# Linear attention and MLP, two layers: rows of M moved as whole words and split at their chunks, late q further ahead, k ahead of G

## The chip, the cores and the metric

The kernel runs on one core of a Trainium2 chip. The metric is the device time of one execution in microseconds. A core has five engines that run side by side, each through its own list of instructions in order: PE (TensorE, matmuls; its weight loads are shown apart as PEld), DVE (VectorE), ACT (ScalarE), POOL (GpSimd) and SP (SyncE, which here issues nearly all transfers). They wait for each other through semaphores. Transfers run on 16 DMA engines. Matmul results land in PSUM, which has eight banks; everything else lies in SBUF.

## The reference

Two layers, each a linear attention block and an MLP, on 2048 rows of width 640 (32 heads of 20), MLP width 1728, in float32:

```python
def _A_ref(x, wqkv, wo):
    q, k, v = ...
    phi = lambda t: jnp.where(t > 0, t + 1, jnp.exp(t)) + 1e-6
    pq, pk = phi(q), phi(k)
    kv = jnp.einsum("bhsd,bhse->bhde", pk, v)
    z = jnp.einsum("bhsd->bhd", pk)
    num = jnp.einsum("bhqd,bhde->bhqe", pq, kv)
    den = jnp.einsum("bhqd,bhd->bhq", pq, z)[..., None] + 1e-6
    ...
    return (num / den).reshape(B, S, D) @ wo

def _B_ref(x, w1, b1, w2, b2):
    h = jnp.einsum("bsd,df->bsf", x, w1) + b1
    r = jnp.where(h > 0, h, 0)
    return jnp.einsum("bsf,fd->bsd", r * r, w2) + b2

x = x + _A_ref(_layernorm(x), wqkv, wo)
x = x + _B_ref(_layernorm(x), w1, b1, w2, b2)
...
```

The last two lines run twice, once for each layer.

## The kernel before

The 2048 rows are 16 tiles of 128 rows. A float32 product is made of three matmuls in the type fp32r: each operand is split into a high part (a copy rounded to fp32r, mostly by ACT) and a low part (the operand less the high part, by DVE), and high by low, low by high and high by high are added up in PSUM (`mm3`, L379). So every operand costs a split, two instructions, before PE can use it.

**The loop over tiles** (L665 to L767) makes k, and for most tiles q, from the turned and normalised x (`part`, 15 matmuls for 320 columns). `Phi` applies the feature map in halves: an exponential on ACT (`exp`, L475) and two operations on DVE (`rest`, L482 and L483). v is never made; instead G = x^T phi(k) is summed over the tiles in five PSUM banks (`g_part`, five parts of three matmuls 512 wide for the tile before, handed out by `gs(n)`), and what doesn't fit there, the last 128 columns, is GT, made for two tiles at a time after every even tile (`gt_part`, two halves of six matmuls, each added into SBUF by DVE, L513). Three banks, XB = 0, 1, 2, serve k, q and GT. Tiles of `LATE` (9, 11 to 15 in layer 0; 8, 9, 11, 13 to 15 in layer 1) leave their q for later: k is made there in two halves, in banks 0 and 1. `k_post` splits phi(k) into kh (high on ACT, low on DVE at L653) and adds it to `acc` on POOL. `move` turns x: DVE turns blocks of 32x32 (L356) and ACT moves them to their places (L365, 16 small moves for a tile). These are also how other tiles are turned later.

**The stage around the change** (from L772). `late_q(n)` makes n of the 12 late parts (half a tile's q each): 15 matmuls, an exponential, the two operations of `rest`, and after a tile's second half a store of it. They fill PE while other engines prepare. Then: G is read out, the small block products per six heads are made (`kv_make`, masked to `kvbd`), and M = (block-diagonal kv) times wo, of 640 by 640, is made in six pieces of 120 rows (`m_make(c)`, c from 0 to 5, the last of 40 rows). PE later needs M in five chunks of 128 rows, so a piece has to move to other partitions: ACT writes the piece's high part (L868), DVE its low part (L869), and SP copies both, 5,120 bytes a row, with up to two transfers into the chunks that the piece crosses (L873, L875). Piece 0 needs no move, its rows are the first of chunk 0; chunk m then gets rows of pieces m and m + 1. Between the pieces the loop gives one entry of `side_work` at a time to ACT (`run_side`: a quarter of the moves that turn a tile of phi(q), or its split into pT), one step of `b_ops` to DVE (`b_step`: phi(q) times z, its sum per head, the division, the turning), and one late part after piece 2.

**Behind the loop** PE makes pT times M for tiles 0 and 1: chunks 0 to 2 of both tiles, then chunks 3 and 4 of both (`proj`). `x_turned(i)` adds the result to x (`b_x1`, L621), normalises and turns it; tiles 2 and 3 follow whole (`b_out`), with late parts between. Tiles 2 and 3 are turned by PE (`f_trans`), and with `f_split` xTb, the operand of the MLP's first product (`fc1`, L987), is complete for the first four tiles. The rest of a layer is the MLP over four groups of four tiles, into which the attention output of later tiles is woven.

Short tiles of 128x640 (`ftile`) share 12 buffers; tiles of both halves (`xtile`: xh, kh, pT, kvbd, and the pieces Mc) share 8 in each layer. The program's order on each engine is the order of the text.

Of the kernel before, what the change touches and what calls it, by code (L numbers as in the profile page):

```python
# [8 lines left out]
F32 = mybir.dt.float32  # L9
R32 = mybir.dt.float32r  # L10
AF = mybir.ActivationFunctionType
ALU = mybir.AluOpType
# [59 lines left out]
def kernel(  # L72
# [25 lines left out]
    def bank(i, n=1):  # L98
        return PS[:, 512 * i : 512 * (i + n)]
# [269 lines left out]
    def halves(ps):  # L369
        return ps.rearrange("p (b n) -> p b n", b=2)[:, :, :HD]  # L370

    def halves_sb(t):
        return t.rearrange("p (b n) -> p b n", b=2)
# [58 lines left out]
    for layer in range(N_LAYERS):  # L432
# [57 lines left out]
        def xtile(name, dtype=R32):  # L490
            return xp.tile([P, 2, D], dtype, tag="x", name=name, bufs=8)
# [12 lines left out]
        def gt_part(p, j, ps):  # L504

            ps, rs = ps[:, :HD], slice(j * HD, (j + 1) * HD)
            for t in (2 * p, 2 * p + 1):
                a, b = kh[t][:, :, DM:], xh[t][:, :, rs]
                mm3(ps, a[:, 0], a[:, 1], b[:, 0], b[:, 1], t % 2 == 0, t % 2 == 1)
            if p == 0:  # L510
                nc.vector.tensor_copy(GT_[:, rs], ps)
            else:
                nc.vector.tensor_tensor(out=GT_[:, rs], in0=ps, in1=GT_[:, rs], op=ALU.add)  # L513
# [151 lines left out]
        for t in range(NT):  # L665
            first = t == 0 and layer == 0
            early = t == 0 and layer > 0
            a_load(t + 3, src)
            if first:
                late_consts()  # L670
            if layer == 0:
                prep.store()
                if 6 <= t < 6 + 2 * DC:
                    keep_kq(*divmod(t - 6, 2))
            if t >= 13:
                b_load_pq(t - 13)
                load_vo(2 * t - 26)
                load_vo(2 * t - 25)
            if first:
                fk, fq = Phi(rtile()), Phi(rtile())  # L680
                for nm, f, pss in (("k", fk, (bank(0), bank(1))), ("q", fq, (bank(2), bank(7)))):
                    w = wk(nm)
                    for c in range(DC):
                        for j in range(2):
                            s = slice(j * HD, (j + 1) * HD)
                            mm3(
                                pss[j][:, :HD], xT[t][:, 0, c, :], xT[t][:, 1, c, :],
                                w[c][:, 0, s], w[c][:, 1, s], c == 0, c == DC - 1,
                            )
                        if nm == "q" and c == 2:  # L690
                            a_trans(1, bank(5, 2))
                            a_stats(2)
                            a_apply(2)
                    for j in range(2):
                        f.exp(j * HD, pss[j][:, :HD])
                    if nm == "k":
                        f.rest()
                xh[t] = split_new(xt[t], "xh")
                k_post(t, fk.r)
                fq.rest()  # L700
                nc.sync.dma_start(pqd[0], fq.r)
                continue
            g = list(range(DC)) if t > 0 else []

            def gs(n):
                for _ in range(min(n, len(g))):
                    g_part(t - 1, g.pop(0))

            if q_end:
                q_end()  # L710
                q_end = None
            is_late = t in late
            f, fq = Phi(rtile()), None if is_late else Phi(rtile())
            n0 = HD if is_late else 512
            ps = part(t, 0, n0, bank(XB[0]))
            gs(0 if t == 1 and layer == 0 else 2)
            move(t + 1)
            f.exp(0, ps)
            if layer == 0 and t == 1:
                a_stats(3)  # L720
                a_trans(2, bank(5, 2))
            if not early and t + 2 < NT:
                a_apply(t + 2)
                yza[t + 2] = blocks_T(xt[t + 2])
            f.rest()
            gt = t % 2 == 0 and t > 0
            if gt and is_late:
                gt_part(t // 2 - 1, 0, bank(XB[2]))
            ps = part(t, n0, D if is_late else 1024, bank(XB[1]))
            if t + 1 in yza:  # L730
                xT_split(t + 1, yza.pop(t + 1)[1])
            if early:
                xT_split(2, yz0[2][1])
            for _ in range(PREP.get(t, 0) if layer == 0 else 0):
                prep.high()
            for _ in range(4):
                prep.low()
            for _ in range(PREP.get(t + 1, 0) if layer == 0 else 0):
                prep.load()
            f.exp(n0, ps[:, : D - n0])  # L740
            if not is_late:
                fq.exp(0, ps[:, D - n0 :])
            f.rest()
            if not is_late:
                fq.rest()
            xh[t] = split_new(xt[t], "xh")
            if gt and not is_late:
                gt_part(t // 2 - 1, 0, bank(XB[0]))
            gs(1)
            if is_late:  # L750
                gs(1)
            else:
                ps = part(t, 1024, 2 * D, bank(XB[2]))
                gs(1)
            k_post(t, f.r, [lambda: a_stats(t + 3)])
            if gt:
                gt_part(t // 2 - 1, 1, bank(XB[2 if is_late else 1]))
            gs(DC)
            if not is_late:

                def q_end(t=t, f=fq, ps=ps):
                    f.exp(1024 - D, ps)
                    f.rest()
                    nc.sync.dma_start(pqd[t], f.r)

            move(t + 2, AHEAD)
# [8 lines left out]
        def late_q(n=1, rest=True):  # L775

            for _ in range(n):
                if not late_parts:
                    return
                t, j = late_parts.pop(0)  # L780
                if j == 0:
                    late_phi[t] = Phi(ftile("rl"))
                late_phi[t].exp(j * HD, part(t, D + j * HD, D + (j + 1) * HD))
                late_todo.append((t, j))
                if rest:
                    late_rest()
# [70 lines left out]
        def m_make(c):  # L857
            mb.append(mb.pop(0))
            ps = bank(mb[-1], 2)
            n, o = head_rows(c), HR * c  # L860
            for j in range(2):
                nc.tensor.matmul(
                    ps[:n, j * 512 : j * 512 + HD], kvbd[c][:n, :n],
                    vo["o", c][:n, j * HD : (j + 1) * HD], start=True, stop=True,
                )
            u = M[0] if c == 0 else xtile("Mc")
            hi, lo, src_ = halves_sb(u[:n, 0]), halves_sb(u[:n, 1]), halves(ps[:n])
            nc.scalar.activation(hi, src_, AF.Copy)  # L868
            nc.vector.tensor_tensor(out=lo, in0=src_, in1=hi.bitcast(F32), op=ALU.subtract)  # L869
            if c > 0:  # L870
                m, r = divmod(o, P)
                k = min(P - r, n)
                nc.sync.dma_start(M[m][r : r + k].bitcast(F32), u[:k].bitcast(F32))  # L873
                if k < n:
                    nc.sync.dma_start(M[m + 1][: n - k].bitcast(F32), u[k:n].bitcast(F32))  # L875

        for c in range(NH):
            kv_make(c)
            if c == 0:
                b_load_pq(3)  # L880
            if c == 1:
                b_load_x(0)
            if c == 3:
                b_load_x(1)
            if c == 2:
                run_side(1)
            if c < 4:
                b_step(2)
        sg.close()
        sm = ExitStack()  # L890
# [2 lines left out]
        )  # L893

        M = [mp.tile([P, 2, D], R32, tag="M", name="uM", bufs=DC) for _ in range(DC)]
        late_q(1)
        b_step(2, 9)
        side_moves(yzp[2], lambda: b_split(2, xtile("pT")))
        xbanks = [0, 1]
        for c in range(NH):  # L900
            m_make(c)
            run_side(1)
            b_step(3)
            if c == 2:
                late_q(1)
        side_moves(yzp[3], lambda: b_split(3, xtile("pT")))

        wu.free = 3
        wu.load_ring()
        late_q(1)  # L910
        run_side(1)

# [6 lines left out]
        for i in range(2):  # L921
            po[i] = bank(4 + 2 * i, 2)
            proj(po[i], pT[i], M, range(3))
            run_side(2)

        def x_turned(i):
# [7 lines left out]
            run_side(1)  # L934
            b_load_x(i + 2)
        x_turned(0)
        late_q(1)
        run_side(2)
        x_turned(1)

# [13 lines left out]
        late_q(1)  # L954
        run_side(9)
        f_trans(2, bank(6, 2))
        late_q(1)
        f_trans(3, bank(4, 2))
        late_q(9)
        sa.close()  # L960

        sb = ExitStack()
# [556 lines left out]
```

## Time and profile before

| | us |
|---|---|
| median of 3 runs (lowest to highest) | 1363.93 (1363.85 to 1364.41) |
| the profiled execution, whole | 1362.51 |
| its span, first to last instruction | 1360.3 |

How the lines below are read. A row of the timeline is: start in us from the span's start, duration in us (of all instructions of the row from the first start to the last end), engine, line of the kernel, operation, output<-inputs by the program's names, the engine's shape, the number of instructions merged, and in brackets how long the engine stood idle before and what ended it. SPq marks a transfer being issued. In a table of waits the three numbers are the total in us, how many times, and the longest. A row of windows gives for a stretch of time the busy us of PE, PEld, DVE, ACT and POOL with their instructions, then the granted clock of PE as a share, the mean busy share of the DMA engines, and GB/s. In the page's groups, the row ends with the group's busy time and mean duration and the idle time before it. "DMA to landing" is from the issue of a transfer to its completion: lowest, median, highest of the group.

### The profile page before, as it was taken

The numbers are of one execution on the slowest core, as the hardware profiler recorded it, in microseconds if no ns is written. First come the engines' busy times: TensorE is split into PE (matmuls) and PEld (weight loads), VectorE is DVE, ScalarE is ACT, GpSimd is POOL, SyncE is SP. The second block draws the span as 40 slices with busy tenths as digits, with TensorE's granted clock in tenths as the row PEclk, the third lists the DMA queues.
The fourth block names the chain that finished last, engine by engine and source line by source line (L and its number), as shares of the span: only waits on it lengthen the run. The fifth ranks groups of instructions, "written<-read, shape, count | busy, mean of one in ns | idle before, by whom it ended". The sixth has DMA issues, their size and how long they took to land.

```text
span 1360.3 us, 19010 instructions
## 1 busy us (share of the span) xinstructions
PE 1344.3 (99%) x6817; PEld 1161.5 (85%) x6817; DVE 910.4 (67%) x1617; ACT 770.8 (57%) x1931; POOL 122.8 (9%) x174
## 2 busy tenths in 40 slices
PE   9999998999999999999999999989999999999998
PEld 8888987988888888888888898978888888888887
DVE  7888766777777676643467676757778667775323
ACT  5888857666646447411447687475756446464110
POOL 2222210000000000000012232100000000000000
PEclk9999999999999999999999999999999999999999
DMA  6787825583664484387521114175546646644834
GB/s 203 252 301 268 285 82 172 200 306 119 230 242 157 160 303 165 113 328 295 183 97 54 44 47 148 40 243 224 183 159 224 223 144 220 249 158 142 290 122 158
DMA packets 85635, 256.10 MB, mean 188 GB/s; under 512 B 11030, under 2 KB 19606, under 8 KB 84902
## 3 DMA queue, kind: packets, MB, share of 16 engines
q1 hardware_dynamic: 85398, 254.70, 53.1%
q8 instruction: 54, 0.88, 0.3%
q14 instruction: 39, 0.32, 0.1%
q10 hardware_dynamic: 144, 0.20, 0.0%
HBM read 193.50 MB, written 56.03 MB: 183 GB/s over the span
## 4 chain that ended last, share of the span: by engine, by line
PE 93%; ACT 3%; DMA 2%; DVE 1%; issue 0%; SPq 0%; POOL 0%; DVEq 0%
PE PS L379 36%; PE PS L987 27%; PE PS L1037 27%; ACT z L365 2%; DMA uM<-Mc 1%; PE PS L849 1%; ACT Mc L868 0%; DMA st<-in_A_wqkv_dram 0%; ACT e L475 0%; PE PS L1051 0%; DVE r L483 0%; DVE kq L128 0%; ACT xTb L127 0%; DVE e L482 0%; ACT kh L646 0%
## 5 line engine op out<-in xcount | busy, mean ns | idle before, releaser
L365 ACT ACTIVATE z<-y 32x160 f32<-32x160 f32 x1424 | 475.8, 334 | 73.8 <-DVE y L356 57.5
L987 PE MATMUL PS<-xTb,u 128*128 128x512 f32 x1400 | 333.8, 390 | 0.6 <-DVE xTb L128 0.6
L987 PEld LDWEIGHTS PS<-xTb,u 128*128 128x128 f32 x1400 | 261.6, 188 | 54.6 <-DVE xTb L128 1.1
L379 PE MATMUL PS<-kq,xT 128*128 128x320 f32 (+2 forms) x1635 | 296.1, 333 | 1.0 <-DVE kq L128 0.9
L379 PEld LDWEIGHTS PS<-kq,xT 128*128 128x128 f32 x1635 | 260.1, 188 | 28.7 <-DVE kq L128 1.1
L1037 PE MATMUL PS<-u,h 128*128 128x512 f32 x1120 | 276.8, 390 | 0.0
L1037 PEld LDWEIGHTS PS<-u,h 128*128 128x128 f32 x1120 | 208.5, 188 | 40.8
L999 ACT ACTIVATE hr<-PS,b1sb 128x512 f32<-128x512 f32 x104 | 71.4, 687 | 296.8 <-PE PS L987 296.1
L1000 DVE TENSOR_TENSOR hr<-hr 128x512 f32<-128x512 f32 x104 | 71.7, 690 | 219.1 <-ACT hr L999 218.5
L379 PE MATMUL PS<-kh,xh 128*128 128x512 f32 x480 | 126.0, 393 | 0.8 <-DVE kh L653 0.8
L475 ACT ACTIVATE e<-PS 128x320 f32<-128x320 f32 (+4 forms) x128 | 53.8, 436 | 115.0 <-PE PS L379 111.8
L379 PE MATMUL PS<-uM,pT 128*128 128x320 f32 x648 | 104.9, 312 | 8.2 <-DMA uM<-Mc 8.2
L379 PEld LDWEIGHTS PS<-uM,pT 128*128 128x128 f32 x648 | 99.3, 190 | 11.0 <-issue 7.9
L340 POOL TENSOR_SCALAR rs<-mv 128x1 f32<-128x1 f32 x64 | 28.2, 441 | 874.9 <-DVE mv L338 874.9
L379 PEld LDWEIGHTS PS<-kh,xh 128*128 128x128 f32 x480 | 86.9, 188 | 16.1 <-DVE kh L653 1.6
L482 DVE TENSOR_SCALAR e<-e 128x320 f32<-128x320 f32 (+4 forms) x128 | 41.1, 321 | 77.4 <-ACT e L475 77.2
L1037 PE MATMUL PS<-h,u 128*128 128x512 f32 x280 | 79.0, 390 | 0.0
L1002 DVE TENSOR_TENSOR h<-hr,h 128x512 fp32r<-128x512 f32 x104 | 72.0, 693 | 3.6
L650 POOL TENSOR_TENSOR acc<-acc,r 128x640 f32<-128x640 f32 x30 | 53.9, 1796 | 204.8 <-DVE r L483 204.8
L1037 PEld LDWEIGHTS PS<-h,u 128*128 128x128 f32 x280 | 52.2, 188 | 10.8 <-DVE h L1013 0.4
L987 PE MATMUL PS<-xTb,uw 128*128 128x512 f32 x240 | 57.0, 389 | 0.0
L483 DVE SCALAR_TENSOR_TENSOR r<-PS,e 128x512 f32<-128x512 f32 (+2 forms) x104 | 51.1, 492 | 5.8 <-ACT e L475 2.4
(119 smaller groups left out, 1336.2 us busy)
## 6 DMA issues: line engine op xcount, KB each, us to landing
u<-kept_w SPq DMA_DIRECT2D x184, 640.0 KB, 4.1
x<-x SPq DMA_DIRECT2D x48, 320.0 KB, 5.1
kept_w<-uprep SPq DMA_DIRECT2D x23, 640.0 KB, 4.5
pqt<-pq SPq DMA_DIRECT2D x32, 320.0 KB, 4.3
x<-xr SPq DMA_DIRECT2D x32, 320.0 KB, 4.1
st<-in_B_w_dram SPq DMA_DIRECT2D x22, 320.0 KB, 5.7
pq<-r SPq DMA_DIRECT2D x20, 320.0 KB
kept_kq<-kq SPq DMA_DIRECT2D x10, 640.0 KB, 6.7
```

Of the source, the lines that this page charges most:

```text
L340: nc.gpsimd.tensor_scalar(rs, mv[:, 1:2], LN_EPS, None, op0=ALU.add)
L365: nc.scalar.activation(zv[j * B32 : (j + 1) * B32, :, i, :], yv[i * B32 : (i + 1) * B32, :, j, :], AF.Copy)
L379: nc.tensor.matmul(ps, a, b, start=first and i == 0, stop=last and i == 2)
L475: nc.scalar.activation(self.e[:, a:b], ps, AF.Exp)
L482: nc.vector.tensor_scalar(e, e, 1.0, PHI_EPS, op0=ALU.min, op1=ALU.add)
L483: nc.vector.scalar_tensor_tensor(out=self.r[:, a:b], in0=ps, scalar=0.0, in1=e, op0=ALU.max, op1=ALU.add)
L650: nc.gpsimd.tensor_tensor(out=acc, in0=acc, in1=r, op=ALU.add)
L987: nc.tensor.matmul(ps, a[:, d, :], bb[:, d, :], start=d == 0 and i == 0, stop=d == DC - 1 and i == len(seq) - 1,)
L999: nc.scalar.activation(r, ps, AF.Relu, bias=b1sb[:, c : c + 1])
L1000: nc.vector.tensor_tensor(out=r, in0=r, in1=r, op=ALU.mult)
L1002: nc.vector.tensor_tensor(out=h[:, 1], in0=r, in1=h[:, 0].bitcast(F32), op=ALU.subtract)
L1037: nc.tensor.matmul(ps, l, r, start=first and k == 0, stop=last and k == len(a) - 1)
```

## The change

Three edits. First, `m_make` no longer splits a piece: ACT copies it as float32 into one tile, and the transfers carry whole words, 2,560 bytes a row, into raw chunks `m_raw` (three tiles of the kind `xtile`, two chunks in each; a piece on its way is now an `ftile`). A new function `m_split(m)` makes chunk m's high part with a copy on DVE and its low part with a subtraction on DVE, once its rows are there. Second, the late parts behind the loop are placed otherwise: two parts, each with one entry of side work and one `m_split`, ahead of the ring's weight loads and of the first product with M; the part behind the first `x_turned` is gone; and the last two parts leave their `rest` until after the splits of x (`late_rest`). `b_step(2)` is called three times instead of four within the loop over `kv_make`. Third, in late tiles the second half of k follows the first directly: no part of G between them, and both halves of GT follow later, the second in bank XB[0] instead of XB[2], ahead of `k_post`.

```diff
-            gs(0 if t == 1 and layer == 0 else 2)
+            gs(0 if is_late or t == 1 and layer == 0 else 2)
...
-            if gt and is_late:
-                gt_part(t // 2 - 1, 0, bank(XB[2]))
             ps = part(t, n0, D if is_late else 1024, bank(XB[1]))
...
             gs(1)
             if is_late:
                 gs(1)
+                if gt:
+                    gt_part(t // 2 - 1, 0, bank(XB[2]))
+                gs(1)
+                if gt:
+                    gt_part(t // 2 - 1, 1, bank(XB[0]))
...
             k_post(t, f.r, [lambda: a_stats(t + 3)])
-            if gt:
-                gt_part(t // 2 - 1, 1, bank(XB[2 if is_late else 1]))
+            if gt and not is_late:
+                gt_part(t // 2 - 1, 1, bank(XB[1]))
...
-            u = M[0] if c == 0 else xtile("Mc")
-            hi, lo, src_ = halves_sb(u[:n, 0]), halves_sb(u[:n, 1]), halves(ps[:n])
-            nc.scalar.activation(hi, src_, AF.Copy)
-            nc.vector.tensor_tensor(out=lo, in0=src_, in1=hi.bitcast(F32), op=ALU.subtract)
+            u = m_raw[0] if c == 0 else ftile("Mc")
+            nc.scalar.activation(halves_sb(u[:n]), halves(ps[:n]), AF.Copy)
             if c > 0:
                 m, r = divmod(o, P)
                 k = min(P - r, n)
-                nc.sync.dma_start(M[m][r : r + k].bitcast(F32), u[:k].bitcast(F32))
+                nc.sync.dma_start(m_raw[m][r : r + k], u[:k])
                 if k < n:
-                    nc.sync.dma_start(M[m + 1][: n - k].bitcast(F32), u[k:n].bitcast(F32))
+                    nc.sync.dma_start(m_raw[m + 1][: n - k], u[k:n])
+
+        def m_split(m):
+            nc.vector.tensor_copy(M[m][:, 0], m_raw[m])
+            nc.vector.tensor_tensor(
+                out=M[m][:, 1], in0=m_raw[m], in1=M[m][:, 0].bitcast(F32), op=ALU.subtract
+            )
...
-            if c < 4:
+            if c < 3:
                 b_step(2)
...
+        m_raw = [xtile("Mr", F32) for _ in range(3)]
+        m_raw = [m_raw[m // 2][:, m % 2] for m in range(DC)]
...
             if c == 2:
                 late_q(1)
+            if c in (3, 4):
+                m_split(c - 3)
         side_moves(yzp[3], lambda: b_split(3, xtile("pT")))
+        late_q(1)
+        run_side(1)
+        m_split(2)
+        late_q(1)
+        run_side(1)
+        m_split(3)
 
         wu.free = 3
         wu.load_ring()
-        late_q(1)
-        run_side(1)
...
             proj(po[i], pT[i], M, range(3))
+            if i == 0:
+                m_split(4)
             run_side(2)
...
         x_turned(0)
-        late_q(1)
         run_side(2)
         x_turned(1)
...
         f_trans(2, bank(6, 2))
-        late_q(1)
+        late_q(1, False)
         f_trans(3, bank(4, 2))
-        late_q(9)
+        late_q(9, False)
+        late_rest()
```

## The prediction

> **What bounds the kernel now.** I read the page first, then the waits of the tensor engine, then the timeline around those waits. The page's first lines:
>
> ```profile
> span 1360.3 us, 19010 instructions
> PE 1344.3 (99%) x6817; PEld 1161.5 (85%) x6817; DVE 910.4 (67%) x1617; ACT 770.8 (57%) x1931; POOL 122.8 (9%) x174
> ```
>
> PE is the bound nearly everywhere. The change gives it the same matmuls as before, so it can only win or add holes. The table of PE's waits names them:
>
> ```profile
> PE PS L379 <- DMA uM<-Mc: 8.2, 4, 2.9
> PE PS L379 <- DVE kh L653: 0.8, 1, 0.8
> PE PS L987 <- DVE xTb L128: 0.6, 2, 0.3
> ```
>
> All three parts of the diff aim at these rows: M not yet in its chunks (8.2 us), kh late (0.8), the turned x late for the first product of the MLP (0.6). The place is the M stage of each layer; layer 0 first, layer 1 in the last three rows:
>
> ```profile
> 220.86 2.47 PE L379 MATMUL PS<-kq,xT 128*128 128x320 f32 x15
> 223.17 1.92 PE L379 MATMUL PS<-uM,pT 128*128 128x320 f32 x12
> 223.17 0.68 ACT L868 ACTIVATE Mc<-PS 40x640 fp32r<-40x640 f32 x1
> 224.04 0.81 DVE L869 TENSOR_TENSOR Mc<-PS,Mc 40x640 fp32r<-40x640 f32 x1
> 225.32 0.77 SPq L873 DMA_DIRECT2D uM<-Mc  x1
> 227.94 4.63 PE L379 MATMUL PS<-uM,pT 128*128 128x320 f32 x30 [2.85 <-DMA uM<-Mc]
> 234.07 2.87 PE L379 MATMUL PS<-uM,pT 128*128 128x320 f32 x18 [1.50 <-DMA uM<-Mc]
> 236.78 2.36 PE L379 MATMUL PS<-kq,xT 128*128 128x320 f32 x15
> 238.98 4.56 PE L379 MATMUL PS<-uM,pT 128*128 128x320 f32 x30
> 892.24 2.46 PE L379 MATMUL PS<-kq,xT 128*128 128x320 f32 x15
> 897.44 4.64 PE L379 MATMUL PS<-uM,pT 128*128 128x320 f32 x30 [0.98 <-DMA uM<-Mc]
> 904.91 4.41 PE L379 MATMUL PS<-uM,pT 128*128 128x320 f32 x18 [2.83 <-DMA uM<-Mc]
> ```
>
> PE multiplies with M[0] and M[1], then stands 2.85 us for M[2] and 1.50 for M[4]. The last piece of Mc is copied by ACT until 223.85, its low half is done at 224.85, its transfer is issued at 225.32 and M[4] is usable at about 234. The 18 matmuls behind the wait last 2.87 us in layer 0 and 4.41 in layer 1; the granted clock (the number behind POOL's, before the DMA share and GB/s) says why:
>
> ```profile
> 224.00:226.00 2.00, 1.09 (x8) 0.82 (x6) 1.35 (x4) 1.93 (x7) 0.00 (x0) 1.00 1.05 232
> 236.00:238.00 2.00, 2.00 (x16) 2.00 (x15) 1.14 (x4) 0.00 (x0) 0.62 (x2) 1.00 1.01 403
> 238.00:242.00 4.00, 4.00 (x29) 4.00 (x28) 2.42 (x5) 2.73 (x7) 0.17 (x1) 1.00 1.04 418
> 906.00:908.00 2.00, 2.00 (x9) 2.00 (x8) 1.53 (x3) 0.00 (x0) 0.00 (x0) 0.50 1.01 410
> ```
>
> In layer 1 the clock was 0.50 after the wait, which cost 4.41 - 2.87 = 1.54 us more. And the DMA engines are full (share 1.05) at 232 GB/s while M moves, against 418 when ordinary loads run: the moves of M are bound by their bytes.
>
> **Part 1, M moved as whole words.** Removed: six subtractions of 0.81 on DVE ahead of the transfers, and half of the bytes. Each transfer goes out right behind ACT's copy, the last at about 223.9 instead of 225.32. Added: five splits, each a rounding copy and a subtraction. The nearest rows:
>
> ```profile
> 265.52 0.43 DVE L1001 CAST h<-hr 128x512 fp32r<-128x512 f32 x1
> 230.39 0.82 DVE L128 TENSOR_TENSOR pT<-z,pT 128x640 fp32r<-128x640 f32 x1 [4.08 <-ACT pT L127]
> DMA to landing us min/median/max: 5.4/6.2/6.9
> pq<-rl SPq DMA_DIRECT2D x12, 320.0 KB, 2.3
> ```
>
> The copy is 0.43 x 640/512 = 0.54 us, so a split is 0.54 + 0.82 = 1.36. DVE stood idle 4.08 us just here, so the splits have room, but they run in DVE's order. Landing lies between 2.3 us (a 320 KB store with free engines) and 6.2 (the moves now); with half the bytes and engines no longer full I take 3.5. What sets the splits is then not landing but what stands ahead of them on DVE, the two results of late q, which come from ACT:
>
> ```profile
> 222.53 0.74 ACT L127 ACTIVATE pT<-z 128x640 fp32r<-128x640 f32 x1
> 223.76 1.36 ACT L365 ACTIVATE z<-y 32x160 f32<-32x160 f32 x4
> 225.02 0.41 ACT L475 ACTIVATE e<-PS 128x320 f32<-128x320 f32 x1
> 225.46 0.33 DVE L482 TENSOR_SCALAR e<-e 128x320 f32<-128x320 f32 x1 [0.61 <-ACT e L475]
> 225.82 0.49 DVE L483 SCALAR_TENSOR_TENSOR rl<-PS,e 128x320 f32<-128x320 f32 x1
> ```
>
> M[0] is split before 222.7. Then DVE waits for the pT that ACT gives at 223.27, subtracts until 224.1, splits M[1] until 225.4, finishes the late part until 226.3, splits M[2] until 227.6. ACT turns four blocks (1.36) and makes the next exponential until 227.25; DVE finishes that part by 228.4, splits M[3] by 229.75 and M[4] by 231.1.
>
> **Part 2, late q in front.** By my count one part more stands ahead of the first product, not two: two behind the loop instead of one, and the one behind the first block's addition is gone. One part is 238.98 - 236.78 = 2.20 us of 15 matmuls, 0.147 each. PE after: late parts until 225.22, M[0] and M[1] (12 matmuls) until 226.98, a wait of 0.7 for M[2] until 227.65, the other 24 to 231.2, M[3] and M[4] without wait, first block done at 232.95, second at 234.7. There the third block starts, which started at 238.98: 4.3 us earlier. This is not kept whole, since DVE's chain to the MLP starts with the first block's addition:
>
> ```profile
> 235.22 0.82 DVE L621 TENSOR_TENSOR xr<-PS,xr 128x640 f32<-128x640 f32 x1 [4.00 <-PE PS L379]
> 246.95 0.79 DVE L621 TENSOR_TENSOR xr<-PS,xr 128x640 f32<-128x640 f32 x1
> 259.45 0.81 DVE L128 TENSOR_TENSOR xTb<-PS,xTb 128x640 fp32r<-128x640 f32 x1
> 260.32 7.12 PE L987 MATMUL PS<-xTb,u 128*128 128x512 f32 x30 [0.29 <-DVE xTb L128]
> 932.69 7.10 PE L987 MATMUL PS<-xTb,u 128*128 128x512 f32 x30 [0.30 <-DVE xTb L128]
> ```
>
> The addition moves from 235.22 to 233.2. From it to the first MLP product there were 25.1 us. Two late parts (0.82 of DVE each) leave this stretch, one moved ahead and one put behind the last split of x; DVE is nearly full from 246.95 on, so I subtract most of both, 1.4 us: 233.2 + 23.7 = 256.9. The ends are 255.75 (PE's own work, 234.7 + 260.03 - 238.98) and 258.3 (the stretch keeps 25.1). Layer 0 wins 260.32 - 256.9 = 3.4 (2.0 to 4.6). Layer 1 stands 892.24 - 220.86 = 671.38 later, so its product comes at 928.3 instead of 932.69: 4.4 (3.0 to 5.6), more because the halved clock goes with the wait.
>
> The Trainium skill (TensorE: Matmul & The Clock Gate, Part 1: The HAM clock gate) says that the clock falls to half when a free-running window of about 3.4 us saw too little work. The trace agrees with 0.50 at 906 us, and the 1.00 at 236 us shows that waits of the same size can miss the window. By that rule a wait of 0.7 us leaves the clock alone; if a halving stayed, the sum would be 1.5 us higher.
>
> **Part 3, k ahead of G in late tiles.**
>
> ```profile
> 162.01 0.81 DVE L128 TENSOR_TENSOR xh<-xt,xh 128x640 fp32r<-128x640 f32 x1
> 163.07 2.36 PE L379 MATMUL PS<-kq,xT 128*128 128x320 f32 x15
> 164.87 0.48 DVE L513 TENSOR_TENSOR GT<-PS,GT 128x320 f32<-128x320 f32 x1
> 174.04 1.64 PE L379 MATMUL PS<-kh,xh 128*128 128x512 f32 x6 [0.77 <-DVE kh L653]
> ```
>
> G of tile 13 comes 2.2 us later in tile 14, so the wait of 0.77 goes. But the second half of GT now lies in the bank in which the next tile's k begins. In tile 12 DVE ends xh at 162.8; both additions to GT, 0.48 each, follow it now, and with k's second part earlier by 0.2 that ends near 163.5, where PE wants the bank at 163.07: about 0.45 us late, twice in layer 0 (tiles 12 and 14). I take 0 for the part, with ends of a gain of 0.8 and a loss of 1.8 (0.45 at all four even late tiles of the two layers, and nothing back).
>
> **Sum.** The profiled execution took 1362.51 us (span 1360.3). Less 3.4 and 4.4: 1354.7. The runs shown have a median 1.42 above it, about the price of one halved window, so I put half of that on: 1355.4.
>
> **The rivals.**
> 1. The stretch to the MLP keeps its length: 2.0 + 3.0 = 5.0 won, 1358.2 with the same half. For it: DVE is nearly full there. Against: work does leave it.
> 2. Transfers keep 6.2 us although halved. Then M[4] lands at 230.1 and is split by 232.3, M[2] by 228.4, so that its wait grows from 0.7 to 1.5: 0.8 us more per layer, 1357.0. Against: share 1.05 at 232 GB/s. The Trainium skill (DMA: Bandwidth & Descriptors, on the two cost components) gives a transfer about 2 us fixed plus its bytes over 436 GB/s, which speaks for this rival: halving 200 KB would be an estimated 0.2 us. The trace differs, 6.2 us with full engines.
> 3. The splits wait in DVE's order as long as the transfers did: nothing won, 1363.9. It needs M[4] at 234, 3 us behind my 231.1.
> 4. Slower: Mc now lives in the ring of 12 short tiles with y, z, e and xr. By my count 11 or 12 are live around the third piece, where ACT makes the exponential of a late part:
>
> ```profile
> 219.35 0.44 ACT L475 ACTIVATE e<-PS 128x320 f32<-128x320 f32 x1
> ```
>
> If its tile is given the place of the piece just sent (issued some 0.7 us before), it waits for that landing, 6.2 - 0.7 = 5.5 us, and with it ACT's remaining copies: M[4] near 231.1 + 5.5 + 1.0 of queue = 237.6, the second block done at 240.3, the MLP 2.1 us later than before in each layer, and a second halving of 1.54: 1362.51 + 4.2 + 1.5, with the same half 1368.9. It decides once the wait on ACT passes about 4 us; under that something is still won. Against: places free for longer exist at that point.
>
> **Chances.** Forecast 0.50, rival 1 0.22, rival 2 0.10, rival 3 0.08, rival 4 0.10. A difference under 0.2% (2.7 us) can't be told from none: faster 0.82, same 0.08, slower 0.10. The range goes from every wait and the halving won, 1362.51 - 8.2 - 1.5 - 0.8 - 0.6 = 1351.4, to just above rival 1 and its neighbours, 1362; it leaves out rivals 3 and 4.
>
> **What would show it.** Right: the row of PE waiting for uM<-Mc gone and one for M's split under 1.5 us in all; ACT's last copy of M near 223.9 and its transfer right behind; the third block at 234 to 235.5, the MLP's first product near 257 and 928; granted clock 1.00 through 909; no wait for kh. Wrong: ACT waiting for a transfer in the loop over M, PE waiting for GT at the head of tiles 13 and 15 by over 1 us, or the MLP waiting more than 1.5 us for xTb.

## The result, and the profile after

| | before, us | after, us |
|---|---|---|
| median of 6 runs each (lowest to highest) | 1364.09 (1363.38 to 1364.55) | 1352.86 (1352.46 to 1353.55) |
| ratio after to before, 95% interval | | 0.9919 (0.9906 to 0.9931) |
| the profiled execution, whole | 1362.51 | 1352.46 |
| its span | 1360.3 | 1350.5 |

The change made the kernel faster by 11.2 us, with the forecast at 1355.4. The page after, its first lines:

```profile
span 1350.5 us, 19013 instructions
PE 1342.5 (99%) x6817; PEld 1160.9 (86%) x6817; DVE 912.1 (68%) x1625; ACT 770.2 (57%) x1931; POOL 122.6 (9%) x174
```

PE has the same 6817 matmuls and DVE eight instructions more, as the splits are now five times two a layer instead of six subtractions. The table of PE's waits (total, times, longest) after, without the start-up rows:

```profile
PE PS L1005 <- DVE xTb L128: 1.0, 2, 0.5
PE PS L379 <- DVE uM L881: 0.7, 2, 0.3
...
PE PS L379 <- DVE GT L513: 0.4, 1, 0.4
```

The 8.2 us for uM from the transfers and the 0.8 for kh are gone. In their place stand 0.7 for the splits, 0.4 for GT, and 1.0 instead of 0.6 for xTb. Rows picked from the timeline of the M stage after, layer 0 and then three rows of layer 1:

```profile
220.18 4.67 PE L379 MATMUL PS<-kq,xT 128*128 128x320 f32 x30
222.49 0.68 ACT L871 ACTIVATE Mc<-PS 40x640 f32<-40x640 f32 x1
223.42 0.77 SPq L875 DMA_DIRECT2D Mr<-Mc  x1
224.68 1.92 PE L379 MATMUL PS<-uM,pT 128*128 128x320 f32 x12
226.07 0.83 DVE L881 TENSOR_TENSOR uM<-Mr,uM 128x640 fp32r<-128x640 f32 x1
226.95 11.70 PE L379 MATMUL PS<-uM,pT 128*128 128x320 f32 x78 [0.34 <-DVE uM L881]
228.83 0.49 DVE L880 CAST uM<-Mr 128x640 fp32r<-128x640 f32 x1
232.53 0.82 DVE L621 TENSOR_TENSOR xr<-PS,xr 128x640 f32<-128x640 f32 x1 [1.51 <-PE PS L379]
255.76 6.63 PE L1005 MATMUL PS<-xTb,u 128*128 128x512 f32 x28 [0.49 <-DVE xTb L128]
...
887.33 4.67 PE L379 MATMUL PS<-kq,xT 128*128 128x320 f32 x30
894.10 11.70 PE L379 MATMUL PS<-uM,pT 128*128 128x320 f32 x78 [0.35 <-DVE uM L881]
922.91 2.33 PE L1005 MATMUL PS<-xTb,u 128*128 128x512 f32 x9 [0.49 <-DVE xTb L128]
```

Two late parts (30 matmuls) now stand ahead of the products with M, one stood there before. Then 12 products, one wait of 0.34 us for the split of M[2], and 78 products in one piece. M[4] begins its split at 228.83, without a wait for its transfer. The time of the moves and three windows (stretch, then PE, PEld, DVE, ACT, POOL, granted clock, DMA share, GB/s):

```profile
DMA to landing us min/median/max: 2.3/2.6/2.8
```

```profile
222.00:224.00 2.00, 2.00 (x16) 2.00 (x15) 1.35 (x3) 1.98 (x5) 0.00 (x0) 1.00 0.50 140
224.00:226.00 2.00, 2.00 (x15) 2.00 (x14) 1.89 (x4) 1.93 (x7) 0.00 (x0) 1.00 0.53 155
906.00:908.00 2.00, 2.00 (x16) 2.00 (x15) 0.97 (x4) 1.94 (x6) 0.79 (x2) 1.00 0.85 337
```

A move lands in 2.6 us instead of 6.2 (the trace has this time for two sizes: 5.4 and 6.9 us for 480 and 160 KB before, 2.8 and 2.3 for 240 and 80 KB after). From 224 to 226 us the DMA engines are half busy (0.53) where they were full (1.05), and the clock at 906 us is 1.00 where it was 0.50.

**Where the 11.2 us came from.** Two marks cut each layer: the first late part behind the loop over tiles, and the first product of the MLP. In layer 0 they stood at 220.86 and 260.32 before, at 220.18 and 255.76 after: 0.68 us come from the loop over tiles and 260.32 - 220.86 - (255.76 - 220.18) = 3.88 from the M stage. In layer 1 the M stage went from 932.69 - 892.24 = 40.45 to 922.91 - 887.33 = 35.58, which is 4.87; the stretch from one layer's MLP to the next layer's M stage, with the other loop over tiles, gave 0.35 (631.92 to 631.57). That is 9.8 us, the difference of the spans. Of the other 1.4, 0.25 lie outside the span (1362.51 - 1360.3 against 1352.46 - 1350.5), and 1.2 are not in these two traces: the timed runs of before have a median 1.58 above their profiled execution, those of after 0.40. What this most likely is, the part on the clock says.

### The profile page after: what moved, and what is told of

It is laid out like the page before. It is cut to its first block, busy times and chain, and to the rows that moved or that the text cites. A ratio compares the mean times of both kernels' runs of the same rounds, so it can differ in the third digit from the quotient of the medians.

```text
span 1350.5 us, 19013 instructions
## 1 busy us (share of the span) xinstructions
PE 1342.5 (99%) x6817; PEld 1160.9 (86%) x6817; DVE 912.1 (68%) x1625; ACT 770.2 (57%) x1931; POOL 122.6 (9%) x174
## 4 chain that ended last, share of the span: by engine, by line
PE 92%; DVE 4%; ACT 3%; issue 1%; POOL 0%; DMA 0%; DVEq 0%; ACTq 0%; POOLq 0%
PE PS L379 34%; PE PS L1005 28%; PE PS L1055 28%; ACT z L365 2%; PE PS L852 1%; PE PS L865 1%; DVE bn L336 0%; PE PS L521 0%; DVE kq L128 0%; DVE e L482 0%; DVE xr L621 0%; DVE r L483 0%; DVE xTb L128 0%; DMA Mr<-Mc 0%; POOL rs L341 0%
```

## The experiments

The "stage" in this table is the M stage as just defined, from the first late part behind the loop to the first MLP product. Each batch of runs had runs of before on the same chip (medians 1363.69, 1364.16 and 1363.70), and each ratio is to those.

| run | median, us | ratio to before (95%) | stage, layer 0 | stage, layer 1 |
|---|---|---|---|---|
| before | 1364.09 | 1 | 39.45 | 40.45 |
| after | 1352.86 | 0.9919 (0.9906 to 0.9931) | 35.58 | 35.58 |
| M alone | 1359.09 | 0.9964 (0.9950 to 0.9978) | 38.99 | 37.47 |
| late q alone | 1357.32 | 0.9955 (0.9943 to 0.9967) | 36.49 | 37.30 |
| k alone | 1361.73 | 0.9988 (0.9979 to 0.9997) | 40.54 | 40.70 |
| full bytes | 1357.45 | 0.9955 (0.9943 to 0.9968) | 37.42 | 37.11 |
| ring later | 1361.67 | 0.9989 (0.9981 to 0.9998) | 40.45 | 40.16 |
| warm | 1361.60 | 0.9985 (0.9976 to 0.9994) | 39.00 | 39.49 |
| second bank of GT | 1357.20 | 0.9954 (0.9942 to 0.9967) | 35.59 | 35.61 |
| rest in place | 1354.33 | 0.9932 (0.9919 to 0.9946) | 36.35 | 36.36 |
| rest later | 1350.29 | 0.9904 (0.9890 to 0.9917) | 34.31 | 34.32 |
| GT first | 1349.59 | 0.9899 (0.9884 to 0.9914) | 34.34 | 34.34 |

### Each edit alone

M alone: the first edit in the kernel before, with the late parts where they were.

```diff
+            if c in (3, 4):
+                m_split(c - 3)
         side_moves(yzp[3], lambda: b_split(3, xtile("pT")))
...
         late_q(1)
         run_side(1)
+        m_split(2)
+        m_split(3)
...
             proj(po[i], pT[i], M, range(3))
+            if i == 0:
+                m_split(4)
```

> The kernel before with the first edit alone: whole words moved, chunks split on DVE, every late part where it was. My theory (M arrives earlier because less is moved and it leaves earlier) expects PE's wait for uM<-Mc gone, waits for the splits instead (M[2] near 227.7, since PE comes to M 2.2 us earlier than in the changed kernel), the third block of the first layer near 237 instead of 238.98, no halved clock in the second layer, and 3 to 6 us less in all. The rival that only the late parts in front win the time expects under 1 us less. The rival that the splits take as long as the transfers expects no change or more.

It won 4.6 us. Its waits and timeline of PE:

```profile
PE PS L379 <- DVE uM L877: 4.6, 4, 1.2
```

```profile
221.10 2.47 PE L379 MATMUL PS<-kq,xT 128*128 128x320 f32 x15
...
225.68 1.15 PE L379 MATMUL PS<-uM,pT 128*128 128x320 f32 x6 [1.23 <-DVE uM L877]
227.87 8.85 PE L379 MATMUL PS<-uM,pT 128*128 128x320 f32 x48 [1.04 <-DVE uM L877]
...
898.82 7.31 PE L379 MATMUL PS<-uM,pT 128*128 128x320 f32 x48 [1.05 <-DVE uM L877]
```

The waits fall from 8.2 to 4.6 and now end with DVE, not with a transfer: without the second late part PE gets to M[1] before DVE has split it. And 48 matmuls take 8.85 us in layer 0, where the same 48 take 7.31 in layer 1: the granted clock was 0.54 and 0.61 in the two windows from 228 to 232 us. So the third block began at 238.75, hardly earlier than before, and not near 237 as expected; the 1.54 us between 8.85 and 7.31 are nearly all of that miss. The time came out as expected, but by way of layer 1 (40.45 to 37.47) more than of layer 0.

Late q alone: the second edit, with M still split ahead of its transfers.

```diff
+        late_q(1)
+        run_side(1)
+        late_q(1)
+        run_side(1)
 
         wu.free = 3
         wu.load_ring()
-        late_q(1)
-        run_side(1)
...
         x_turned(0)
-        late_q(1)
...
```

> The kernel before with the second edit alone: the late parts placed as in the changed kernel, M moved and split as before. My theory expects M[4] to come at about 234 as before, since nothing in M's path changed: a late part fills some of the waits, the third block starts near 236.8 and the MLP of the first layer some 1.4 us earlier, 2 to 4 us less in all. The rival that the late parts alone win the time expects 7 us or more less.

It won 6.4 us, more than expected.

```profile
PE PS L379 <- DMA uM<-Mc: 3.4, 2, 2.1
```

```profile
221.63 4.66 PE L379 MATMUL PS<-kq,xT 128*128 128x320 f32 x30
226.13 6.32 PE L379 MATMUL PS<-uM,pT 128*128 128x320 f32 x42
233.74 7.27 PE L379 MATMUL PS<-uM,pT 128*128 128x320 f32 x48 [1.28 <-DMA uM<-Mc]
...
902.99 7.27 PE L379 MATMUL PS<-uM,pT 128*128 128x320 f32 x48 [2.08 <-DMA uM<-Mc]
```

The part in front covers the wait for M[2] whole (42 products run through), and no late part of 2.20 us stands between M[4] and the third block any more. In layer 0 M[4] is there 233.74 - 221.63 = 12.1 us after the first late part, where it took 234.07 - 220.86 = 13.2 before; in layer 1 it came no earlier (902.99 - 890.08 = 12.9 against 904.91 - 892.24 = 12.7), but the 1.54 us of the halved window are gone, as this profile has none. The expectation counted only the matmuls moved in front; it had neither the earlier M[4] in layer 0 nor the clock. The edit also puts the ring's weight loads behind another late part; whether that brought M[4] earlier, the next run asks. (Its expectation has 11.97 for the 12.1 of the rows above.)

Ring later: only the loads of the ring moved behind the late part, in the kernel before.

```diff
-        wu.free = 3
-        wu.load_ring()
         late_q(1)
         run_side(1)
+        wu.free = 3
+        wu.load_ring()
```

> The kernel before with one order changed: the ring's weight loads are issued behind the late part that follows the loop over M and behind its store, as the second edit does, and no late part is moved. In the second edit alone M[4] came 11.97 us after the first late part behind the loop instead of 13.21 (first layer), though nothing in M's own path changed. If that is the weight loads keeping out of M's way, M[4] comes 0.5 to 1.3 us earlier here too and the kernel is 1 to 2.5 us faster. The rival that M[4] only varies from run to run expects no difference beyond 0.8 us.

The medians are 2.0 us apart, with an interval from 0.3 to 2.6. In layer 0 M[2] is usable 226.21 - 220.66 = 5.6 us after the first late part, where it took 7.1, and M[4] 12.7 instead of 13.2:

```profile
220.66 2.46 PE L379 MATMUL PS<-kq,xT 128*128 128x320 f32 x15
...
226.21 4.63 PE L379 MATMUL PS<-uM,pT 128*128 128x320 f32 x30 [1.32 <-DMA uM<-Mc]
233.33 4.41 PE L379 MATMUL PS<-uM,pT 128*128 128x320 f32 x18 [2.49 <-DMA uM<-Mc]
```

That the order of the loads did this is not shown. K alone, the next run, leaves the loads and the moves of M as they were before, and has the same times in layer 0:

```profile
221.09 2.47 PE L379 MATMUL PS<-kq,xT 128*128 128x320 f32 x15
...
226.64 4.63 PE L379 MATMUL PS<-uM,pT 128*128 128x320 f32 x30 [1.32 <-DMA uM<-Mc]
233.86 4.41 PE L379 MATMUL PS<-uM,pT 128*128 128x320 f32 x18 [2.58 <-DMA uM<-Mc]
```

Here M[2] comes 226.64 - 221.09 = 5.6 us after the first late part and M[4] 12.8. In layer 1 M[4] took 12.4 us in ring later, 12.7 before and 12.9 in k alone. So the rival that M[4] varies from run to run stands, and what brought M[4] at 12.1 us in layer 0 of late q alone stays open. The stage of layer 0 is no shorter for the earlier M[4], since the 18 matmuls behind it take 4.41 us: this profile has a halved window in layer 0, which the profile of before has not. The 0.54 us by which M[4] came earlier and the 1.54 of the window give 39.45 - 0.54 + 1.54 = 40.45 for the stage, as measured. The 2.0 us between the medians are in part the clock: only 4 of the 11 runs had a mean clock of 0.997 or less, against 29 of the 45 runs of before. Among runs of 0.998 the means are 0.6 us apart, among those of 0.997 1.2.

K alone: the third edit, in the kernel before.

```diff
-            if gt and is_late:
-                gt_part(t // 2 - 1, 0, bank(XB[2]))
...
+                if gt:
+                    gt_part(t // 2 - 1, 0, bank(XB[2]))
+                gs(1)
+                if gt:
+                    gt_part(t // 2 - 1, 1, bank(XB[0]))
```

> The kernel before with the third edit alone: k ahead of G in late tiles. From the trace of the changed kernel, 0.68 us in the first layer and about 0.35 in the second: 0.7 to 1.3 us less, with a wait of about 0.4 us for GT at the head of tile 15 of the first layer. My prediction had 0 for it. The rival that this edit only shifts waits about expects no difference.

It won 2.0 us with an interval from 0.4 to 2.9. In the trace the loops over tiles show only 0.59 in layer 0, counted from PE's last wait of the start-up (ended at 16.13 before and at 16.94 here), and 0.33 on the way to layer 1. Runs of equal mean clock agree with that: at 0.998 the mean time is 0.9 us under that of before, at 0.997 0.6. The rest of the 2.0 fits halved windows met less often (8 of 11 runs at 0.998 or more, 16 of 45 before); this is inferred from the clocks. The wait for kh is gone from PE's table and one for GT of 0.4 us has come, at the head of tile 15. Its profiled execution had a second halved window (stage of layer 0: M[4] comes 0.44 earlier, so 39.45 - 0.44 + 1.54 = 40.55, measured 40.54).

### The bytes

Full bytes: the kernel after, with rows of 5,120 bytes again. The second half of a row carries M as float32, the first half a filler that POOL writes early; everything else stays, the splits behind the landing too. ACT writes its copy rounded to the type fp32r, so that M's low part is zero.

```diff
-            u = m_raw[0] if c == 0 else ftile("Mc")
-            nc.scalar.activation(halves_sb(u[:n]), halves(ps[:n]), AF.Copy)
+            u = M[0] if c == 0 else mc[c]
+            nc.scalar.activation(halves_sb(u[:n, 1]), halves(ps[:n]), AF.Copy)
...
-                nc.sync.dma_start(m_raw[m][r : r + k], u[:k])
+                nc.sync.dma_start(M[m][r : r + k].bitcast(F32), u[:k].bitcast(F32))
```

> The changed kernel, but each piece is moved as 5,120 bytes a row again, with as many transfers, issued as early as in the changed kernel, and with the same splits on DVE; half of the bytes moved are filler that POOL writes beforehand. The raw words are rounded to fp32r by ACT here, so M's low part comes out zero. If the halved bytes are what brings M earlier (the engines were full at 232 GB/s), M[4] comes 3 us or more later than with half the bytes, PE waits for it, and the kernel is 2 to 4.5 us slower than the changed one, that is 7 to 9 us under the kernel before. If it is the issue without a subtraction ahead of it, the time is that of the changed kernel within 1 us.

It is 4.6 us slower than after (3.9 between the two profiles' spans), of which 3.4 are in the two stages (1.84 and 1.53).

```profile
DMA to landing us min/median/max: 5.8/5.9/6.1
```

```profile
222.00:224.00 2.00, 2.00 (x16) 2.00 (x15) 1.36 (x3) 1.96 (x5) 0.00 (x0) 1.00 1.02 207
```

```profile
232.22 0.49 DVE L881 CAST uM<-uM 128x640 fp32r<-128x640 f32 x1 [2.67 <-DMA uM<-Mc]
233.63 6.57 PE L379 MATMUL PS<-uM,pT 128*128 128x320 f32 x43 [1.58 <-DVE uM L882]
```

The engines are full again (1.02 at 207 GB/s), a move takes 5.9 us by the same two sizes, and DVE, which after began M[4] without a wait, stands 2.67 us for it. M[4]'s last move, issued at 224.16, lets DVE begin at 232.22, 8.1 us later. So the landing time follows the bytes; the earlier issue and the later splits alone do not give it.

### The clock

Warm: the kernel before, with transposes of the identity into a free bank while PE waits for M[2] and for M[4]. The waits stay; only the clock can gain.

```diff
+        def fill(n):
+            for _ in range(n):
+                nc.tensor.transpose(bank(3)[:, :P], ident, ident)
...
-            proj(po[i], pT[i], M, range(3))
+            proj(po[i], pT[i], M, range(2))
+            if i == 0:
+                fill(7)
+            proj(po[i], pT[i], M, (2,))
...
-            proj(po[i], pT.pop(i), M, range(3, DC))
+            proj(po[i], pT[i], M, (3,))
+            if i == 0:
+                fill(12)
+            proj(po[i], pT.pop(i), M, (4,))
```

> The kernel before with nothing but filler added: 7 transposes of the identity into a free bank ahead of M[2] and 12 ahead of M[4], 109 ns each, less than the waits that stand there. In the timed runs of before the mean granted clock lies mostly at 0.997, in its profile at 0.998, in the changed kernel at 1.000; a halved window of 3.4 us takes 0.00125 off. If these windows are part of what the waits cost, the fillers raise the clock to 0.999 or more and win 1.5 to 3 us, and the waits in the profile keep their sum with the fillers in them. The rival that the clock has other reasons expects the same clock and time within 1 us.

The gain is 2.6 us (interval 0.8 to 3.3). Layer 1:

```profile
891.82 2.47 PE L379 MATMUL PS<-kq,xT 128*128 128x320 f32 x15
...
901.99 1.47 PE L923 MATMUL PS<-ident 128*128 128x128 f32 x12
905.04 2.88 PE L379 MATMUL PS<-uM,pT 128*128 128x320 f32 x18 [1.58 <-DMA uM<-Mc]
```

M[4] comes 13.2 us after the first late part, 0.55 later than before, yet the stage is 0.96 shorter: the 18 matmuls take 2.88 instead of 4.41. In all eleven runs the mean clock was 0.999 or 1.000; in 29 of the 45 runs of before beside the experiments it is 0.997 or less, and 0.998 in its profile. The profiles of ring later and of k alone, at 0.997, have a halved window in each layer. One is 1.54 us or 0.11% of the span, so most timed runs of before have, by their clock, one window more than the profile that the prediction was made against. That fits the 1.58 between the two, and the mean times of the runs at 0.997 and at 0.998, 2.0 us apart; it is inferred from the clocks, as these runs have no traces. The six runs of after all have 1.000.

### The order of DVE and of the banks

Rest in place: the kernel after, with the last late parts finished where they are made.

```diff
-        late_q(1, False)
+        late_q(1)
         f_trans(3, bank(4, 2))
-        late_q(9, False)
-        late_rest()
+        late_q(9)
```

> The changed kernel with the last two late parts finished on DVE where they were before, ahead of the splits of x. My prediction counted about 0.7 us per layer for each late part that leaves DVE's stretch between the first block's addition and the MLP: the wait for xTb grows from 0.49 to about 1.3 in each layer, 1.2 to 1.8 us slower. The rival that the late parts there are hidden expects the same time within 0.4 us.

```profile
PE PS L1004 <- DVE xTb L128: 2.5, 2, 1.3
```

```profile
256.94 5.30 PE L1004 MATMUL PS<-xTb,u 128*128 128x512 f32 x22 [1.25 <-DVE xTb L128]
```

It costs 1.5 us, 0.77 in each stage. Two parts' `rest` are put back ahead of the splits of x, of 0.33 + 0.49 = 0.82 us of DVE each, so the stage pays for about one of the two. DVE is what the MLP waits for here.

Rest later: the kernel after, with three more late parts whose `rest` is postponed, so that the splits of M[2] and M[3] stand ahead of them.

```diff
-        late_q(1)
+        late_q(1, False)
         run_side(1)
         m_split(2)
-        late_q(1)
+        late_rest()
+        late_q(1, False)
         run_side(1)
         m_split(3)
+        late_rest()
...
-        late_q(1)
+        late_q(1, False)
         run_side(9)
```

> The changed kernel with three more results of late q put behind work that PE waits for: M[2] and M[3] are split ahead of the late parts' operations on DVE, and the third last late part leaves its operations until after the splits of x too. By my theory DVE's order is what is left: the waits for M's split (0.34 twice) and for xTb (0.49 twice) go, 1 to 2.3 us less than the changed kernel. The rival that M[2] has not landed earlier and that DVE's stretch to the MLP is as long in any order expects the same time within 0.5 us.

```profile
224.74 13.36 PE L379 MATMUL PS<-uM,pT 128*128 128x320 f32 x90
...
254.55 7.00 PE L1007 MATMUL PS<-xTb,u 128*128 128x512 f32 x30
```

The 90 products run without a hole, the waits for uM and for xTb are gone, and the kernel is 2.6 us under after.

Second bank of GT: the kernel after, with GT's second half in the bank of the first.

```diff
-                    gt_part(t // 2 - 1, 1, bank(XB[0]))
+                    gt_part(t // 2 - 1, 1, bank(XB[2]))
```

> The changed kernel with the second half of GT in late tiles back in bank XB[2], behind the first half. The wait of 0.41 us for GT at the head of tile 15 goes, but then PE has to wait for the first half's addition before the second half starts, which in tile 14 of the first layer ends near 180.3 us where the second half starts at 177.98 now, and in tile 12 near 162.2 against 160.44: 2 to 4 us slower than the changed kernel. The rival that the other bank costs nothing expects 0.4 us less.

```profile
PE PS L379 <- DVE GT L513: 3.9, 4, 1.6
```

```profile
162.80 1.14 PE L379 MATMUL PS<-xh,kh 128*128 128x320 f32 x6 [1.65 <-DVE GT L513]
```

It is 4.3 us slower than after: with one bank for both halves, the second half waits for DVE's addition of the first in every even late tile, up to 1.65 us. With the next tile's k bank, as in the change, only 0.41 once is left.

GT first: rest later, with the split of xh behind both additions to GT in even late tiles.

```diff
-            xh[t] = split_new(xt[t], "xh")
+            if not (gt and is_late):
+                xh[t] = split_new(xt[t], "xh")
...
                     gt_part(t // 2 - 1, 1, bank(XB[0]))
+                    xh[t] = split_new(xt[t], "xh")
```

> The changed kernel with the late parts' results put behind PE's work as in e6_rest_later, and with the split of x for G in even late tiles put behind both additions to GT. The wait of 0.41 us for GT at the head of tile 15 of the first layer goes, since DVE adds 0.8 us sooner, and nothing else moves: 0.3 to 0.8 us less than e6_rest_later. The rival that the split is then late for G, or that ACT's order turns worse, expects the same or more.

Its median is 0.7 us lower, and the wait for GT (0.41) is gone; PE now waits only at the start. The two kernels ran in different batches, and against their own runs of before they are 13.9 and 14.1 us faster, so the times alone don't tell them apart. At 1349.59 us this has the lowest median of the kernels.

## Why the prediction was right, and where it was off

The forecast was 1355.4, the time 1352.86; against the profiled execution, 1354.7 was the sum and 1352.46 the time. Step by step, with 0.68 taken off the predicted places, since layer 0's stage begins that much earlier:

- **Late parts in front, splits in DVE's order: right.** The products with M begin at 224.68 (predicted 224.54), M[2] at 226.95 (226.97), the first addition at 232.53 (232.52), the third block at 234.09 (234.02; measured as the next late part's 238.49 less the 4.40 that a block takes). One late part more stands in front, not two. PE waited 0.34 us for M[2] instead of 0.7, because it came to M[1]'s end a little later.
- **Landing: too long, without effect.** 3.5 us taken, 2.6 measured. Neither sets the splits, as the prediction said. Rival 2 (6.2 us in spite of half the bytes) is refuted by the trace, and its condition was made in the run with full bytes: it cost 1.84 and 1.53 us of stage, not 0.8. The rival took the median for M[4]'s last move too, which came 8.1 us after its issue there (and 234.07 - 225.32 = 8.8 before), so that DVE stands at M[4] with everything behind it. (Its 232.3 for M[4]'s split is also 0.4 later than its own chain, 228.4 + 0.82 + 1.36 + 1.36, without effect on its time.) The figure worked out in the prediction from the Trainium skill (DMA: Bandwidth & Descriptors, on the two cost components), 0.2 us for half the bytes, does not fit: 160 KB landed in 6.9 us before and in 5.8 in the run with full bytes, with the DMA share up to 1.05, and 80 KB in 2.3 after, at 0.50 to 0.53.
- **The stretch to the MLP: mis-sized by 0.47 in each layer.** Taken from 25.1 to 23.7, it went to 255.76 - 232.53 = 23.2. So 1.9 us left it where 1.4 was taken for two late parts of 0.82. The postponed `rest`s account for 0.77 of that (rest in place); the other 1.1, put down to the part moved ahead, was not tried by itself. Rival 1 (the stretch keeps its length) fell: the MLP began at 255.76, close to the end that the prediction gave for PE's own work (255.75, or 255.07 with the 0.68 off), and DVE held PE up by 0.49 us only.
- **The halved clock of layer 1: right; the half window for the median: wrong.** The profile after shows 1.00 at 906 us. What failed is the half window that was added because the timed runs of before stood above their profile: it should have been none. The prediction itself had the halved clock go with the wait, and after, all six runs have a mean clock of 1.000. That is 0.71 us too much.
- **Part 3: mis-sized.** Taken as 0, with a gain of 0.8 as its best end, the loops gave 0.68 + 0.35 = 1.03 us. The wait for kh (0.77) went as said. The counter-cost was mis-sized: 0.45 us after each of tiles 12 and 14 was expected, and 0.41 came once only, ahead of tile 15's k. These two waits make 0.36; the other 0.67 stands in no row of the tables of waits and was not traced further. The rows of the counter-cost:

```profile
162.73 4.63 PE L379 MATMUL PS<-kq,xT 128*128 128x320 f32 x30
...
180.81 4.64 PE L379 MATMUL PS<-kq,xT 128*128 128x320 f32 x30 [0.41 <-DVE GT L513]
```

- **Rivals 3 and 4 fell.** M[4] was being split at 228.83, not at 234. ACT's last copy ran from 222.49 to 223.17 and its transfer was issued at 223.42, as predicted with the 0.68 off, so no short tile made ACT wait.

These terms make up the difference: 2 x 0.47 of the stretch, 0.71 of the half window and 1.03 of part 3, with 0.25 outside the span and less the 0.40 that the median of after stands above its profile, are 2.5 us, which is 1355.4 - 1352.86.

The three edits alone won 4.6, 6.4 and 2.0 us, 12.9 in all, where together they won 11.2. They need not add up: the halved windows, worth 2.6 us in the timed runs of before by the run with fillers, are there to be won once, and each of the first two edits takes some of them. The two also need each other in another way: with M alone PE waits for the splits, with late q alone for the transfers (4.6 and 3.4 us), and together for 0.7.

## What to carry to other kernels

Where DMA engines are full, move the fewest bytes and split or convert at the destination, provided the engine that splits has room and the consumer can be given other work first; here the order of the late parts alone won 6.4 us and the move as whole words alone 4.6. Operations on an engine with a due split behind them belong behind it if their own consumer is far away: the two `rest`s postponed in the change were worth 1.5 us, three more 2.6. When timed runs stand above their own profile by a fixed step, compare their mean clocks with the profile's and look for a halved window in the waits before costing anything against that profile, and ask whether the change removes it.

## What the runs showed of the hardware

- Halving the bytes of a move between partitions more than halved its time: rows of 5,120 bytes ran at 207 to 232 GB/s with the DMA share at 1.02 to 1.05 in the windows shown, and landed in 5.9 to 6.2 us (median); rows of 2,560 bytes landed in 2.6 us at a share of 0.50 to 0.53 with 140 to 155 GB/s. The last move of M took longer than the median: 8.1 and 8.8 us from its issue until M[4] could be used.
- The size of a wait alone does not tell whether the clock halves. Late q alone stood 2.08 us in layer 1 and had no slow stretch in its profile; M alone stood 1.23 and 1.04 us in layer 0 and had one (granted clock 0.54 and 0.61), and 1.24 and 1.05 us in layer 1 and had none. The waits of before halved the clock in one layer of its profile and in both layers of the profiles of k alone and of ring later. 7 and 12 short transposes in the two waits were enough to keep the mean clock at 0.999 or 1.000 in eleven runs. The Trainium skill (TensorE: Matmul & The Clock Gate, Part 1: The HAM clock gate) has the window free-running, and these numbers agree with that, without proving it.
